# A routing table made in smaller pieces beside four expert tiles instead of three

## The chip, the cores and the metric

The kernel runs on one core of one Trainium2 chip. The metric is device microseconds from launch to end. The engines are called PE (TensorE, the matrix engine), DVE (VectorE), ACT (ScalarE), POOL (GpSimd) and SP (SyncE, which here only issues DMAs). Each takes its own instructions in order.

## The reference

A spectral layer on 8 sequences of 2496 x 256, then a mixture of 8 experts, one expert per token, 19968 tokens in all:

```
X  = rfft(x, axis=1)
Yr = Xr @ w_r - Xi @ w_i + b_r ;  Yi = Xr @ w_i + Xi @ w_r + b_i
Y  = soft-shrink of both by 0.01 ;  y = irfft(Y)           # 8 x 2496 x 256
logits = y @ w_gate ;  expert = argmax(logits) ;  g = softmax(logits)[expert]
out[token] = g * (relu(y @ w1[expert]) @ w2[expert])       # w1 256x1024, w2 1024x256
```

## The kernel before, in words

**Spectral part** (`spectral`, 80 iterations, ten for each of 8 batches). An iteration multiplies, shrinks and transforms one slice of frequencies of its batch (`fwd_b`, `halves`, `mix`, `shrink`, `inv_b`; one copy `k`, L349, in each), and in four of the ten also runs three steps of the last transform of the batch before (`inv_a`, matmuls `pz` and `py`). In the last batch there is no next batch to begin. `finish_last` then runs `inv_a` for the last batch alone.

**Routing** (`route`). For each half of a batch some 25 small DVE operations and a few others find every token's expert and its row in `xs_dram`, a list sorted by expert; eleven scatters by POOL (L637) then write the tokens there. This is a Python generator: the code between two `yield`s is a piece. The generators wait in `self.jobs`, one behind the other, and `tick(n)` runs the next n pieces of the first one at the place where it is called. `send(n)` does the same with the scatters, each behind a one-element copy by POOL (`pace`, L568).

**Tables** (`table`). An expert tile is 256 rows of `xs_dram` of one expert. `table(0)` chooses, from the counts without the last two batches, five early tiles (`EARLY`); it is queued after the second iteration of the last batch. `table(1)` lists the remaining tiles when all tokens are routed. Each is a chain of some 36 DVE operations on 128 x 8 values, two small groups of matmuls (`pn`, `pq`; `pl` for the second) and a cast into `tabs`, from which SP reads a tile's row, expert and whether the expert changed (`word`, L748).

**Expert tiles** (`step(t)` = `up(t)`, then `down(t)`). `up` multiplies the tile's tokens by `w1` into four groups `ph`; ACT makes `hh` of each (L863) and DVE `hl` (L864), the two halves of an exact split. After each group one piece of `upright(t + 1)` is run, which turns the next tile's tokens: for early tiles by PE (`px`, L828), for the others by a DVE transpose (L832) of `xq`, then a cast `xh` by ACT and a subtraction `xl` by DVE. `down` multiplies by `w2` into `po`, half by half, and DVE writes `o` (L904), which POOL scatters to `out`. In its first half `down(t)` splits the `w2` of tile t + 1 (`split2`, L813 on ACT and L814 on DVE) and then asks for that of tile t + 2; in its second half the same with `w1` (`split1`, L798, L799). `load(t)` asks for a tile's rows: four DMAs `xq` and one `xr` on SP. A weight DMA is skipped by a condition where the expert did not change; at the first tile of a table it is always made.

Before the change steps 0 to 2 run in `finish_last`, and `up` and `down` call `tick(3)` after each group of `ph` and each half while `t < 3`: 18 pieces for each tile. Then `experts_rest` asks for the rows of tiles 5 and 6, and in the loop from tile 3 on for those of tile t + 4 ahead of step t. The order of the code is the order on all four engines PE, ACT, DVE and SP (`manual_schedule`).

Of the kernel before, what the change touches and what calls it, by code (L numbers as in the profile page):

```python
# [98 lines left out]
class Kernel:  # L99
# [443 lines left out]
    def finish_last(self, late):  # L543
        for i in range(GH + 1):
            self.inv_a(self.nb - 1, i)
            if self.early and i >= 2:
                next(self.fill, None)
            if self.early and i == GH - 1:
                for _ in self.upright(0):
                    pass  # L550
            self.tick(4)
            if i > GH // 2 + 1:
                self.pace(self.yb[0:1, 0, 8:9])
                self.send(1)
        self.jobs.append(self.table(1))
        if not self.early:
            self.tick(100)
            return
        for _ in self.fill:
            pass  # L560
        for t in range(3):
            self.step(t)
        self.tick(100)
        self.send(100)
# [86 lines left out]
    def table(self, last):  # L651
        nc, rt = self.nc, self.rt
        tcol, base = self.tcol, self.base

        def small(nm):
            return rt.tile([128, E], F32, tag=nm, name=nm)

        def prefix(src):
            a, b = small("pfa"), small("pfb")
            nc.vector.tensor_copy(a, src)  # L660
            for d in (1, 2, 4):
                nc.vector.tensor_copy(b[:, :d], a[:, :d])
                nc.vector.tensor_add(b[:, d:], a[:, d:], a[:, :E - d])
                a, b = b, a
            return a

        p = self.psi.tile([128, 512], F32, tag="yo", name="pn")
        nc.tensor.matmul(p[:, :E], self.ones_b, self.carry_b, start=True, stop=True)
        n8 = small("n8")
        nc.vector.tensor_copy(n8, p[:, :E])  # L670
        cnt = small("cnt")
        half = (TT - 1) / 2
        nc.vector.tensor_scalar(out=cnt, in0=n8, scalar1=half if last else -half, scalar2=1.0 / TT,
                                op0=ALU.add, op1=ALU.mult)
        nc.vector.tensor_scalar_add(cnt, cnt, ROUND)
        nc.vector.tensor_scalar_add(cnt, cnt, -ROUND)
        yield
        te, ge, st0, ind = small("te"), small("ge"), small("st0"), small("ind")
        if last:
            nc.vector.tensor_sub(cnt, cnt, self.used)  # L680
        end = prefix(cnt)
        yield
        nc.vector.tensor_sub(st0, end, cnt)
        fin = rt.tile([128, 5], F32, tag="fin", name="fin")
        for j in range(2):
            nc.vector.tensor_tensor(out=te, in0=tcol[:, j:j + 1].broadcast_to((128, E)), in1=end, op=ALU.is_ge)
            if j == 0:
                nc.vector.tensor_copy(ge, te)
            nc.vector.tensor_reduce(out=fin[:, j:j + 1], in_=te, axis=AX.X, op=ALU.add)
        yield  # L690
        nc.vector.tensor_scalar_min(fin[:, 0:2], fin[:, 0:2], float(E - 1))
        nc.vector.tensor_tensor(out=fin[:, 2:3], in0=fin[:, 0:1], in1=fin[:, 1:2], op=ALU.is_gt)
        nc.vector.tensor_max(fin[:, 1:2], fin[:, 2:3], tcol[:, 2:3])
        nc.vector.tensor_scalar(out=te, in0=st0, scalar1=tcol[:, 0:1], scalar2=-1.0, op0=ALU.subtract, op1=ALU.mult)
        nc.vector.scalar_tensor_tensor(out=ind, in0=te, scalar=0.0, in1=ge, op0=ALU.is_ge, op1=ALU.subtract)
        yield
        nc.vector.tensor_add(te, te, self.used)
        nc.vector.tensor_copy(fin[:, 4:5], end[:, E - 1:E])
        if not last:
            nc.vector.tensor_scalar(out=st0, in0=st0, scalar1=-1.0, scalar2=float(self.early),  # L700
                                    op0=ALU.mult, op1=ALU.add)
            nc.vector.tensor_scalar_max(st0, st0, 0.0)
            nc.vector.tensor_tensor(out=self.used, in0=st0, in1=cnt, op=ALU.min)
        nc.vector.tensor_scalar_add(n8, n8, -float(TT))
        nc.vector.tensor_scalar_mul(te, te, float(TT))
        nc.vector.tensor_tensor(out=st0, in0=te, in1=n8, op=ALU.min)
        nc.vector.tensor_sub(te, te, st0)
        yield
        nc.vector.tensor_mul(te, te, ind)
        nc.vector.tensor_reduce(out=fin[:, 3:4], in_=te, axis=AX.X, op=ALU.add)  # L710
        nc.vector.tensor_add(st0, st0, base)
        nc.vector.tensor_mul(st0, st0, ind)  # L712
        nc.vector.tensor_reduce(out=fin[:, 2:3], in_=st0, axis=AX.X, op=ALU.add)
        for _ in range(6):
            yield
        yield "pe"
        p = self.psi.tile([128, 512], F32, tag="yo", name="pq")
        for i, j in enumerate((0, 1, 2, 4)):
            nc.tensor.matmul(p[0:1, i * 128:(i + 1) * 128], fin[:, j:j + 1], self.ident, start=True, stop=True)
        yield  # L720
        nc.vector.tensor_copy(self.tabs[last], p[0:1, :].rearrange("p (a b) -> p a b", a=4))
        if last:
            lap = rt.tile([128, 128], F32, name="lap")
            nc.vector.tensor_copy(lap, fin[:, 3:4].broadcast_to((128, 128)))
            for _ in range(4):
                yield
            p = self.psi.tile([128, 512], F32, tag="yo", name="pl")
            nc.tensor.matmul(p[:, 0:128], lap, self.ident, start=True, stop=True)
            for h in range(2):
                nc.vector.tensor_scalar(out=self.drop[:, :, h], in0=p[:, 0:128], scalar1=tcol[:, 3 + h:4 + h],  # L730
                                        scalar2=float(OOB), op0=ALU.is_gt, op1=ALU.mult)
# [112 lines left out]
    def up(self, t, work=()):  # L844
        work = iter(work)
        nc = self.nc
        xh, xl = self.xts.pop(t)
        h1, l1 = self.ws.pop((t, 1))
        hh = self.w2p.tile([128, 8, TT], F32R, tag="hh", name="hh")
        hl = self.w2p.tile([128, 8, TT], F32R, tag="hl", name="hl")  # L850
        for f2 in range(4):
            p = (self.psb if self.psb and f2 % 2 else self.psa).tile([128, 2, TT], F32, tag="h", name="ph")
            for i in range(2):
                f = f2 * 2 + i
                m = 0
                for c in range(2):
                    for a, v in ((h1, xh), (l1, xh), (h1, xl)):
                        nc.tensor.matmul(p[:, i, :], a[:, c, f * 128:(f + 1) * 128], v[:, c, :],  # L858
                                         start=m == 0, stop=m == 5)
                        m += 1  # L860
            s = slice(f2 * 2, f2 * 2 + 2)
            with self.tc.high_priority():
                nc.scalar.activation(hh[:, s, :], p, AF.Relu)  # L863
                nc.vector.scalar_tensor_tensor(out=hl[:, s, :], in0=p, scalar=0.0, in1=hh[:, s, :],  # L864
                                               op0=ALU.max, op1=ALU.subtract)
            next(work, None)
            if t < 3:
                self.tick(3)
                self.pace(hh.bitcast(F32)[0:1, f2 * 2, 0:1])
                self.send(1)  # L870
        self.hs[t] = (hh, hl)

    def down(self, t):
# [13 lines left out]
        for h in range(2):  # L887
# [8 lines left out]
                nc.tensor.matmul(p, hh[:, f, hs], w2[:, f].rearrange("p a d -> p (a d)"), start=f == 0, stop=f == 7)  # L896
            for _ in work[h]:
                pass
            if t < 3:
                self.tick(3)  # L900
                self.send(2)
            part = self.w2p.tile([128, D], F32, tag="part", name="part", bufs=2)
# [30 lines left out]

    def experts_rest(self, late):
        late.enter_context(self.tc.manual_schedule(engines={mybir.EngineType.Activation, mybir.EngineType.DVE}))
        t0 = 3 if self.early else 0
        if not t0:
            for _ in self.fill:
                pass
# [43 lines left out]
```

## Time and profile before

| what | value |
|---|---|
| timed runs, median of 3 | 1584.38 us (1581.14 to 1585.53) |
| profiled execution, its own time | 1573.86 us |
| its span, first to last instruction | 1572.1 us |
| busy share PE / DVE / ACT / POOL | 97 / 79 / 69 / 35% |
| mean granted clock of the PE | 0.988 |
| spectral part, last batch, `finish_last` | to about 588, to about 617 us |
| expert tiles | from about 617 us on, 82 of them |

The profiled execution was 10.5 us faster than the median of the timed ones, so a prediction is made as a difference. The page gives busy time by engine and in 40 slices; the granted clock is a share of 2.4 GHz. In the profile's groups a line can stand for many instructions. A wait is put down to what was released last.

### The profile page before, as it was taken

The numbers are of one execution on the slowest core, as the hardware profiler recorded it, in microseconds if no ns is written. First come the engines' busy times: TensorE is split into PE (matmuls) and PEld (weight loads), VectorE is DVE, ScalarE is ACT, GpSimd is POOL, SyncE is SP. The second block draws the span as 40 slices with busy tenths as digits, with TensorE's granted clock in tenths as the row PEclk, the third lists the DMA queues.
The fourth block names the chain that finished last, engine by engine and source line by source line (L and its number), as shares of the span: only waits on it lengthen the run. The fifth ranks groups of instructions, "written<-read, shape, count | busy, mean of one in ns | idle before, by whom it ended". The sixth has DMA issues, their size and how long they took to land. (4 is left out here: it accounts for less than half of the span.)

```text
span 1572.1 us, 36022 instructions
## 1 busy us (share of the span) xinstructions
PE 1523.4 (97%) x10954; PEld 1405.3 (89%) x10954; DVE 1242.6 (79%) x2680; ACT 1078.8 (69%) x2257; POOL 542.4 (35%) x532
## 2 busy tenths in 40 slices
PE   6999999999999898999999999999999999999996
PEld 3899999999999788889999999999999999999996
DVE  3678777777878777788888888888888888888886
ACT  2667677767777566566767677676767676777765
POOL 1002433525253353623343333333333333333333
PEclk8999999999999999999999999999999999999998
DMA  8764545646453113243214123214123123223110
GB/s 245 227 191 125 159 142 146 178 116 186 122 166 109 59 55 124 79 103 101 48 46 102 45 52 93 55 42 103 44 50 96 48 48 96 52 73 71 42 49 20
DMA packets 182964, 153.56 MB, mean 98 GB/s; under 512 B 120474, under 2 KB 154176, under 8 KB 182509
## 3 DMA queue, kind: packets, MB, share of 16 engines
q1 hardware_dynamic: 162829, 107.17, 26.7%
q0 software_dynamic: 19936, 44.04, 8.6%
q8 instruction: 89, 1.46, 0.4%
q14 instruction: 110, 0.90, 0.2%
HBM read 243.07 MB, written 66.37 MB: 197 GB/s over the span
## 5 line engine op out<-in xcount | busy, mean ns | idle before, releaser
L906 POOL DMA_INDIRECT out<-o,row x154 | 302.5, 1965 | 572.3 <-DVE o L904 531.8
L896 PE MATMUL po<-h,hh 128*128 128x512 f32 x1312 | 462.4, 396 | 0.0
L858 PE MATMUL ph<-xh,h 128*128 128x256 f32 x1312 | 371.5, 283 | 0.9 <-ACT h L798 0.7
L858 PE MATMUL ph<-xh,l 128*128 128x256 f32 x1312 | 371.0, 283 | 0.7 <-DVE l L799 0.7
L858 PE MATMUL ph<-xl,h 128*128 128x256 f32 x1312 | 370.6, 282 | 0.0
L863 ACT ACTIVATE hh<-ph 128x512 fp32r<-128x512 f32 x328 | 196.0, 598 | 239.7 <-PE ph L858 222.3
L864 DVE SCALAR_TENSOR_TENSOR hl<-ph,hh 128x512 fp32r<-128x512 f32 x328 | 226.8, 691 | 138.5 <-ACT hh L863 127.7
L893 PE MATMUL po<-h,hl 128*128 128x256 f32 x1148 | 322.2, 281 | 2.5 <-DVE st L712 1.3
L896 PEld LDWEIGHTS po<-h,hh 128*128 128x128 f32 x1312 | 241.6, 188 | 44.7 <-issue 0.6
L858 PEld LDWEIGHTS ph<-xh,l 128*128 128x128 f32 x1312 | 250.8, 191 | 4.8 <-DVE l L799 1.1
L858 PEld LDWEIGHTS ph<-xh,h 128*128 128x128 f32 x1312 | 250.6, 191 | 2.1 <-ACT h L798 1.3
L858 PEld LDWEIGHTS ph<-xl,h 128*128 128x128 f32 x1312 | 250.8, 191 | 0.0
L893 PEld LDWEIGHTS po<-h,hl 128*128 128x128 f32 x1148 | 217.1, 189 | 7.0 <-DVE st L712 1.6
L799 DVE TENSOR_TENSOR l<-r,h 128x512 fp32r<-128x512 f32 x332 | 206.9, 684 | 3.2 <-ACT h L798 2.5
L814 DVE TENSOR_TENSOR h<-r,h 128x512 fp32r<-128x512 f32 x332 | 207.1, 685 | 2.4 <-ACT h L813 2.4
L637 POOL DMA_INDIRECT xs_dram<-yb,pos x176 | 178.2, 1013 | 73.9 <-issue 49.9
L813 ACT CAST h<-r 128x512 fp32r<-128x512 f32 x332 | 180.4, 618 | 1.8 <-DMA r<-moe_w 1.8
L798 ACT CAST h<-r 128x512 fp32r<-128x512 f32 x332 | 180.7, 618 | 1.4 <-DMA r<-moe_w 1.4
L370 DVE SCALAR_TENSOR_TENSOR y<-v,r 64x256 f32<-64x256 f32 x320 | 134.2, 419 | 6.9 <-ACT r L364 1.6
L326 DVE TENSOR_TENSOR su<-re,pb 128x256 f32<-128x256 f32 x80 | 33.7, 421 | 86.9 <-ACT sh L325 42.7
L394 PE MATMUL pz<-iw,z 128*120 128x136 f32 x704 | 97.4, 282 | 0.8 <-ACT z L386 0.7
L903 ACT ACTIVATE part<-po,xr 128x256 f32<-128x256 f32 x154 | 73.1, 475 | 36.1 <-PE po L896 35.9
(183 smaller groups left out, 2813.2 us busy)
## 6 DMA issues: line engine op xcount, KB each, us to landing
r<-moe_w SPq DMA_DIRECT2D x178, 512.0 KB
r<-moe_w SPq DMA_DIRECT2D x632, 128.0 KB
spec_dram<-ae SPq DMA_DIRECT2D x88, 240.0 KB
t<-spec_dram SPq DMA_DIRECT2D x160, 128.0 KB
xq<-xs_dram SPq DMA_DIRECT2D x312, 64.0 KB
x<-x SPq DMA_DIRECT2D x40, 384.0 KB
x<-x SPq DMA_DIRECT2D x40, 84.0 KB
xs_dram<-yb,pos POOLq DMA_INDIRECT x176
```

The source lines that it names most:

```text
L370: nc.vector.scalar_tensor_tensor(out=y[q * 64:q * 64 + 64, kp, :], in0=u[h, q, :], scalar=LAM, in1=r[h, q, :], op0=ALU.add, op1=ALU.min)
L637: i = nc.gpsimd.indirect_dma_start(out=self.xs[:, :], out_offset=bass.IndirectOffsetOnAxis(ap=pos[:n, g:g + 1], axis=0), in_=y[:n, g, 0:XW ...
L798: nc.scalar.copy(hi[:, c, s], v)
L799: nc.vector.tensor_sub(lo[:, c, s], v, hi[:, c, s])
L813: nc.scalar.copy(hi[:, s, :], v)
L814: nc.vector.tensor_sub(lo[:, s, :], v, hi[:, s, :])
L858: nc.tensor.matmul(p[:, i, :], a[:, c, f * 128:(f + 1) * 128], v[:, c, :], start=m == 0, stop=m == 5)
L863: nc.scalar.activation(hh[:, s, :], p, AF.Relu)
L864: nc.vector.scalar_tensor_tensor(out=hl[:, s, :], in0=p, scalar=0.0, in1=hh[:, s, :], op0=ALU.max, op1=ALU.subtract)
L893: nc.tensor.matmul(p[:, :D], hl[:, f - 1, hs], w2[:, f - 1, 0, :], start=False, stop=False)
L896: nc.tensor.matmul(p, hh[:, f, hs], w2[:, f].rearrange("p a d -> p (a d)"), start=f == 0, stop=f == 7)
L906: i = nc.gpsimd.indirect_dma_start(out=self.out[:, :], out_offset=bass.IndirectOffsetOnAxis(ap=at[h], axis=0), in_=o[:, h, :], in_offset=N ...
```

## The change

`table` gets more `yield`s: six ahead of its first operation, one between every one to three operations of the chain, and one in each step of the prefix sum, which becomes a generator itself. Nothing of what is computed changes. So that the table still ends in time, a fourth step is run in `finish_last`, `up` and `down` call `tick` while `t < 4`, and `experts_rest` starts at tile 4.

```diff
@@ finish_last
-        for t in range(3):
+        for t in range(4):
             self.step(t)
@@ table
             for d in (1, 2, 4):
+                yield
                 nc.vector.tensor_copy(b[:, :d], a[:, :d])
...
+        for _ in range(6):
+            yield
         p = self.psi.tile([128, 512], F32, tag="yo", name="pn")
...
                                 op0=ALU.add, op1=ALU.mult)
+        yield
         nc.vector.tensor_scalar_add(cnt, cnt, ROUND)
...
-        end = prefix(cnt)
+        end = yield from prefix(cnt)
...
             nc.vector.tensor_reduce(out=fin[:, j:j + 1], in_=te, axis=AX.X, op=ALU.add)
-        yield
+            yield
         nc.vector.tensor_scalar_min(fin[:, 0:2], fin[:, 0:2], float(E - 1))
         nc.vector.tensor_tensor(out=fin[:, 2:3], in0=fin[:, 0:1], in1=fin[:, 1:2], op=ALU.is_gt)
+        yield
         nc.vector.tensor_max(fin[:, 1:2], fin[:, 2:3], tcol[:, 2:3])
...
@@ up, down
-            if t < 3:
+            if t < 4:
                 self.tick(3)
@@ experts_rest
-        t0 = 3 if self.early else 0
+        t0 = 4 if self.early else 0
```

(The further `yield`s in `table` are of the same kind. Lines of the changed kernel from the table on are 1 to 12 higher.)

What stands where, first on DVE in the last batch of the spectral part, at the start of `table(0)` (L670 to L689 are the table, the others the spectral work of that iteration: `zl` of the transform, `sl` and `y` of the slice). Before:

```order
L330 TENSOR_TENSOR sl_7518<-su_7520,sh_7517 128x2x128
L670 COPY n8_7545<-pn_7543 128x8
L673 TENSOR_SCALAR cnt_7547<-n8_7545 128x8
L675 TENSOR_SCALAR cnt_7547<-cnt_7547 128x8
L676 TENSOR_SCALAR cnt_7547<-cnt_7547 128x8
L660 COPY pfa_7555<-cnt_7547 128x8
...
L686 TENSOR_TENSOR te_7551<-tcol_79,pfb_7556 128x8
L689 TENSOR_REDUCE fin_7565<-te_7551 128x1
L370 SCALAR_TENSOR_TENSOR y_7584<-v_7500,r_7539 64x256 x2
```

Now:

```order
L370 SCALAR_TENSOR_TENSOR y_7556<-v_7500,r_7539 64x256 x2
L673 COPY n8_7592<-pn_7590 128x8
L676 TENSOR_SCALAR cnt_7594<-n8_7592 128x8
L679 TENSOR_SCALAR cnt_7594<-cnt_7594 128x8
L680 TENSOR_SCALAR cnt_7594<-cnt_7594 128x8
L357 TENSOR_TENSOR v_7613<-pm_7598,k_7550 128x512
L400 TENSOR_TENSOR zl_7619<-pz_7615,zh_7618 120x272
L400 TENSOR_TENSOR zl_7626<-pz_7622,zh_7625 120x272
L660 COPY pfa_7643<-cnt_7594 128x8
L663 COPY pfb_7644<-pfa_7643 128x1
L664 TENSOR_TENSOR pfb_7644<-pfa_7643 128x7
L326 TENSOR_TENSOR su_7663<-re_7662,pb_7655 128x256
```

The seventeen rows that stood ahead of `y` are now behind it, in groups with the iterations' own work between them.

On DVE in tile 1, at the start of `table(1)` (`hl` is the tile's own work, L680 to L713 the table's). Before:

```order
L864 SCALAR_TENSOR_TENSOR hl_9178<-ph_9219,hh_9177 128x512
L841 TENSOR_TENSOR xl2_9200<-px_9194,xh2_9199 128x512
L680 TENSOR_TENSOR cnt_9211<-cnt_9211,used_74 128x8
...
L695 SCALAR_TENSOR_TENSOR ind_9238<-te_9235,ge_9236 128x8
L864 SCALAR_TENSOR_TENSOR hl_9178<-ph_9265,hh_9177 128x512
L697 TENSOR_TENSOR te_9235<-te_9235,used_74 128x8
...
L713 TENSOR_REDUCE fin_9250<-st0_9237 128x1
L864 SCALAR_TENSOR_TENSOR hl_9178<-ph_9295,hh_9177 128x512
```

Now:

```order
L876 SCALAR_TENSOR_TENSOR hl_9174<-ph_9227,hh_9173 128x512
L673 COPY n8_9244<-pn_9242 128x8
L676 TENSOR_SCALAR cnt_9246<-n8_9244 128x8
L876 SCALAR_TENSOR_TENSOR hl_9174<-ph_9252,hh_9173 128x512
L679 TENSOR_SCALAR cnt_9246<-cnt_9246 128x8
...
L664 TENSOR_TENSOR pfb_9275<-pfa_9274 128x7
L826 TENSOR_TENSOR h2_9301<-r20_8470,h2_9301 128x2x256
```

Two of the table's rows stand between the tile's pieces of `hl`, the others in groups of three to eight among the splits of the weights; the last twelve come in tile 2, and the cast into `tabs` (`tab1`) at the end of tile 2 instead of tile 1.

On SP after the last weights of the early tiles (`r10`, `r11` are `w1`, `r20`, `r21` are `w2`, `xq` a tile's rows; `xq_9658` and `xq_9837` are those of tile 5). Before:

```order
L786 DMA r11_8473<-moe_w1 128x1024
L763 DMA xq_9658<-xs_dram 32x8x64
...
L763 DMA xq_9674<-xs_dram 32x8x64
...
L763 DMA xq_9690<-xs_dram 32x8x64
...
L786 DMA r20_8474<-moe_w2 128x4x256
L786 DMA r21_8475<-moe_w2 128x4x256
L786 DMA r10_8472<-moe_w1 32x1024
```

Now:

```order
L798 DMA r11_8469<-moe_w1 128x1024
L798 DMA r20_8470<-moe_w2 128x4x256
L798 DMA r21_8471<-moe_w2 128x4x256
L798 DMA r10_8468<-moe_w1 32x1024
...
L798 DMA r11_8469<-moe_w1 32x1024
...
L775 DMA xq_9837<-xs_dram 32x8x64
...
L775 DMA xq_9885<-xs_dram 32x8x64
```

The ten weight DMAs of tile 5, which stood behind the rows of tiles 5 to 7, now stand ahead of the rows of tiles 5 to 8.

## Rows read from the trace of the kernel before

**Rows 1.** The page: busy time by engine, share of the span, instructions.

```profile
PE 1523.4 (97%) x10954; PEld 1405.3 (89%) x10954; DVE 1242.6 (79%) x2680; ACT 1078.8 (69%) x2257; POOL 542.4 (35%) x532
```

**Rows 2.** Busy time by stretch: from:to in us, its length, busy us of each engine (instructions), granted clock of the PE, DMA share, GB/s. The first is an iteration of the batch before the last, the next three of the last batch (from one copy `k` to the next); then tiles 1, 2, 3 and 4, each from one second `o` to the next.

```profile
472.54:481.69 9.15, 9.15 (x74) 8.66 (x73) 7.43 (x25) 6.62 (x20) 0.00 (x0) 1.00 0.21 58
516.10:525.19 9.09, 4.13 (x36) 3.90 (x34) 5.15 (x16) 2.90 (x8) 6.56 (x9) 0.95 0.46 139
525.19:537.19 12.00, 11.44 (x73) 10.83 (x74) 9.85 (x44) 6.27 (x17) 3.61 (x6) 0.75 0.08 26
537.19:547.91 10.72, 10.05 (x81) 9.36 (x79) 7.35 (x20) 6.53 (x19) 0.00 (x0) 1.00 0.00 0
...
630.14:648.97 18.83, 15.83 (x95) 12.46 (x93) 15.65 (x57) 7.80 (x16) 13.91 (x17) 0.91 0.28 87
648.97:660.49 11.52, 11.51 (x79) 10.61 (x80) 9.48 (x17) 7.81 (x15) 8.91 (x11) 1.00 0.20 60
660.49:672.29 11.80, 11.80 (x86) 11.09 (x85) 8.97 (x17) 7.95 (x15) 3.13 (x3) 1.00 0.48 101
672.29:686.54 14.25, 12.83 (x86) 11.23 (x85) 9.85 (x17) 8.14 (x15) 1.96 (x2) 1.00 0.70 186
```

**Rows 3.** The timeline: start, duration, engine, line, operation, in brackets the idle time of the engine just before it and what ended it. Around `table(0)`; last, a stretch as in rows 2.

```profile
519.97 0.37 ACT L324 COPY re<-pb 128x256 f32<-128x256 f32 x1 [3.41 <-PE pz L394]
523.91 0.16 DVE L670 COPY n<-pn 128x8 f32<-128x8 f32 x1
525.62 0.57 PE L408 MATMUL py<-zh,gh 120*117 120x272 f32 x1 [5.39 <-ACT k L349]
529.95 0.16 DVE L711 TENSOR_TENSOR st<-st,base 128x8 f32<-128x8 f32 x1
...
526.00:528.00 2.00, 2.00 (x11) 2.00 (x11) 1.80 (x10) 0.91 (x3) 0.99 (x1) 0.50 0.00 0
```

**Rows 4.** The timeline of tile 1 around `table(1)`; last, two stretches.

```profile
638.15 0.39 PE L893 MATMUL po<-h,hl 128*128 128x256 f32 x1 [1.25 <-DVE hl L864]
639.08 0.17 DVE L709 TENSOR_TENSOR te<-te,ind 128x8 f32<-128x8 f32 x1
640.56 0.58 PE L893 MATMUL po<-h,hl 128*128 128x256 f32 x1 [1.29 <-DVE st L712]
648.12 0.67 DVE L721 CAST tab<-pq 1x512 int32<-1x512 f32 x1
648.72 0.20 DVE L724 COPY lap<-fin 128x128 f32<-128x128 f32 x1
...
640.00:642.00 2.00, 1.44 (x5) 0.92 (x6) 2.00 (x4) 0.77 (x2) 1.66 (x2) 0.59 0.19 61
642.00:644.00 2.00, 2.00 (x10) 1.09 (x9) 0.91 (x2) 0.00 (x0) 1.50 (x1) 0.55 0.21 66
```

**Rows 5.** The timeline of a steady tile, from its start at the second `o` of the tile before to its own.

```profile
731.65 0.48 DVE L904 SCALAR_TENSOR_TENSOR o<-po,xr,part 128x256 f32<-128x256 f32 x1
733.41 0.70 DVE L832 STREAM_TRANSPOSE xf<-xq 128x512 f32<-128x512 f32 x1
734.15 0.62 ACT L838 CAST xh<-xf 128x512 fp32r<-128x512 f32 x1
735.05 0.60 ACT L863 ACTIVATE hh<-ph 128x512 fp32r<-128x512 f32 x1 [0.28 <-PE ph L858]
736.29 0.68 DVE L841 TENSOR_TENSOR xl<-xf,xh 128x512 fp32r<-128x512 f32 x1
737.12 0.69 DVE L864 SCALAR_TENSOR_TENSOR hl<-ph,hh 128x512 fp32r<-128x512 f32 x1 [0.15 <-ACT hh L863]
737.24 0.28 PE L893 MATMUL po<-h,hl 128*128 128x256 f32 x1
738.65 0.28 PE L893 MATMUL po<-h,hl 128*128 128x256 f32 x1
743.01 0.48 DVE L904 SCALAR_TENSOR_TENSOR o<-po,xr,part 128x256 f32<-128x256 f32 x1
```

**Rows 6.** The timeline of SP's queue (start, time until the last of the group was issued) and of ACT's waits for the weights of tile 5; the last two rows are SP's in a steady tile.

```profile
672.59 8.57 SPq L786 DMA_DIRECT2D r<-moe_w  x10
677.72 3.44 SPq L786 DMA_DIRECT2D r<-moe_w  x6
680.59 1.14 ACT L813 CAST h<-r 128x512 fp32r<-128x512 f32 x2 [1.76 <-DMA r<-moe_w]
681.97 1.87 SPq L763 DMA_DIRECT2D xq<-xs_dram  x4
684.08 1.66 ACT L798 CAST h<-r 128x512 fp32r<-128x512 f32 x3 [0.78 <-DMA r<-moe_w]
...
739.31 6.13 SPq L786 DMA_DIRECT2D r<-moe_w  x10
746.06 1.86 SPq L763 DMA_DIRECT2D xq<-xs_dram  x4
```

**Rows 7.** The timeline: POOL's last scatter of the spectral part, SP's loads of the early tiles' rows, and the PE's first use of them.

```profile
593.91 0.90 POOL L637 DMA_INDIRECT xs_dram<-yb,pos  x1 [0.30 <-issue]
599.07 5.42 SPq L758 DMA_DIRECT2D xw<-xs_dram  x5
613.86 0.60 PE L828 MATMUL px<-ident,xw 128*128 128x128 f32 x4
```

More of the change, by code (lines that the diff above doesn't have):

```diff
@@ L689, in table @@
             nc.vector.tensor_reduce(out=fin[:, j:j + 1], in_=te, axis=AX.X, op=ALU.add)
-        yield
+            yield
         nc.vector.tensor_scalar_min(fin[:, 0:2], fin[:, 0:2], float(E - 1))
         nc.vector.tensor_tensor(out=fin[:, 2:3], in0=fin[:, 0:1], in1=fin[:, 1:2], op=ALU.is_gt)
+        yield
         nc.vector.tensor_max(fin[:, 1:2], fin[:, 2:3], tcol[:, 2:3])
         nc.vector.tensor_scalar(out=te, in0=st0, scalar1=tcol[:, 0:1], scalar2=-1.0, op0=ALU.subtract, op1=ALU.mult)
+        yield
         nc.vector.scalar_tensor_tensor(out=ind, in0=te, scalar=0.0, in1=ge, op0=ALU.is_ge, op1=ALU.subtract)
@@ L698, in table @@
         nc.vector.tensor_copy(fin[:, 4:5], end[:, E - 1:E])
+        yield
         if not last:
@@ L702, in table @@
             nc.vector.tensor_scalar_max(st0, st0, 0.0)
+            yield
             nc.vector.tensor_tensor(out=self.used, in0=st0, in1=cnt, op=ALU.min)
         nc.vector.tensor_scalar_add(n8, n8, -float(TT))
+        yield
         nc.vector.tensor_scalar_mul(te, te, float(TT))
         nc.vector.tensor_tensor(out=st0, in0=te, in1=n8, op=ALU.min)
+        yield
         nc.vector.tensor_sub(te, te, st0)
@@ L710, in table @@
         nc.vector.tensor_reduce(out=fin[:, 3:4], in_=te, axis=AX.X, op=ALU.add)
+        yield
         nc.vector.tensor_add(st0, st0, base)
         nc.vector.tensor_mul(st0, st0, ind)
+        yield
         nc.vector.tensor_reduce(out=fin[:, 2:3], in_=st0, axis=AX.X, op=ALU.add)
@@ L898, in down @@
                 pass
-            if t < 3:
+            if t < 4:
                 self.tick(3)
```

## The prediction

> **What bounds the kernel now.** I read the page first. TensorE (PE) is busy for 97% of the span, so an edit counts only where it opens or closes a gap on PE [rows 1]. Then the busy time by stretch. The steady expert tiles show the floor: from one last write of `o` (L904) to the next, 731.65 to 743.01, 11.36 us pass [rows 5]. Below I call the moment at which tile t's last `o` starts T(t). Against this floor three places stand out, and the change touches all of them.
>
> The first is the last batch of the spectral part, where table(0) is made. An iteration, counted from one copy of `k` (L349) to the next, takes 9.15 us with the PE busy for all of it in the batch before, and 12.00 and 10.72 us in the last batch [rows 2]. VectorE (DVE) works off the table there, from the copy `n` at 523.91 us to the operation at 529.95 and a little beyond. The PE has a gap of 5.39 us up to 525.62 and then is granted 0.50 of its clock, the level of 1.2 GHz [rows 3]. But look at the order of events: the PE's last matmul before the gap starts by 520, and ScalarE (ACT) is already late at 519.97, four microseconds before the table's first DVE row. So this gap did not start with the table, and I count it apart.
>
> The second is tile 1, with table(1): 18.83 us, DVE busy for 15.65 of them [rows 2]. Here the cause is plain. Two pieces of `hl` (L864) stand behind runs of table rows, and the PE waits 1.25 us for the one, 1.29 us under the name of a table row for the other, and then is granted 0.59 and 0.55 of its clock on the mean of two stretches [rows 4]. The third is tile 4, 14.25 us: ScalarE waits for the weights of tile 5, which SP began to issue at 672.59 us only, after T(3), since the rows of tiles 5 to 7 stand ahead of them in its queue [rows 2, 6].
>
> **The change part by part.**
>
> *Table(0) in pieces.* The same 36 DVE rows are issued, each some 0.17 us, 0.2 us from one to the next where each needs the one before [rows 3, 4]. They now stand between the pieces of four iterations, in groups of two to eight rows. What they add, 7 us over four iterations of about 9, fits: DVE is busy for 7.43 us of such an iteration [rows 2]. The gain at the two iterations is (12.00 - 9.15) + (10.72 - 9.15) = 4.4 us. In the iteration before them the PE stands idle for 9.09 - 4.13 = 4.96 us [rows 2]. These began before the table and I do not count them; with them the gain would be 9.4 us, the upper end. The lower end is nothing: DVE does the same work, and the routing behind it is pushed into later, shorter iterations.
>
> *The scatters behind it.* The routing of batch 6 now comes later by the table's added turns, so that ten of its scatters stand in one burst at the end of the spectral part instead of five. The burst is hidden: the early tiles' rows were loaded at 599.07 us, after the last scatter (593.91 us), and the PE first used them at 613.86 us. That is 14.8 us of cover, against 5.42 us for issuing the five loads [rows 7]. If the spectral part ends 9 us earlier and the burst does not, the cover is still 5.8 us. Cost 0.
>
> *Table(1) in pieces.* In tile 1 the PE is idle for 18.83 - 15.83 = 3.0 us [rows 2]. The half clock behind its two waits cost, at 0.59 and 0.55 of the clock over 2 us each, another 2 x 0.41 + 2 x 0.45 = 1.7 us [rows 4]. So at most 4.7 us can come back. Is there room for it on DVE? Twelve of the table's rows move to tile 2 (12 x 0.17 = 2.0 us), and the cast of the table and the copy `lap` (0.67 + 0.20 us) with them, 2.9 us [rows 4]. That leaves tile 1 with 15.65 - 2.9 = 12.75 us of DVE work against 15.83 - 1.7 = 14.1 us of PE work, and tile 2 with 9.48 + 2.9 = 12.4 us against the PE's 11.51 and the table's last matmuls, which come along [rows 2]. DVE is thus close to the bound in tile 2, and I leave about 1 us lost in small waits there: 3.7 us gained. The lower end is 1.25 us, one of the two waits; a loss would need table rows in longer runs than before, and the runs get shorter.
>
> *The fourth tile called early.* Step 3 itself costs the same: it has two score buffers for `ph` in place of four, and tile 2, which had two, took 11.52 us against 11.80 us of tile 3, which had four [rows 2]. What moves is its queue work. In its second half it asks for the weights of tile 5, ten DMAs on SP, and the rows of tiles 5 to 8 come behind them. Two things follow. The stall of tile 4, 14.25 - 11.36 = 2.9 us, goes, since the weights are asked for on time. But the rows of tile 5 are now issued after T(3), and DVE's transpose of them (L832) stands in its queue right behind the first `hl` of tile 4, with three more pieces of `hl` behind it. In the steady state this transpose starts at T + 1.76 us (733.41), and the PE uses the second `hl` at T + 5.59 (737.24) and the last one at T + 7.00 (738.65) [rows 5]. From a late transpose at T + X the chain to the last `hl` is 0.70 + 0.62 + 0.60 + 0.69 + 0.68 + 0.69 = 3.98 us (transpose, ACT's cast and `hh`, `hl`, `xl`, `hl`), so the PE is late by X - 3.0 us.
>
> X is in no row. In the steady state the ten weight DMAs are through SP at T + 2.43 (739.31 + 6.13) and the four loads of rows at T + 3.05 to 4.91 [rows 6]; but there the weights are skipped. Where they really were fetched, six issues took 3.44 us and the rows came 0.81 us later; by these, eight from T - 0.5 end at T + 4.1 and the rows are issued by T + 6.8. The nearest row for landing is the last part of `w1`: issued by 681.16, its consumer released at 684.08, 2.9 us [rows 6]. So X lies between 7.8 and 9.7 and I take 8.7: late by 5.7 us. A gap of that size brings the half clock, as the 5.39 us gap did [rows 3]; I take the 1.7 us that it cost in tile 1. Tile 4 thus changes by 5.7 + 1.7 - 2.9 = 4.5 us for the worse. Lower end: rows there the moment they are issued, X = 4.9 and no drop of the clock, a gain of 1.0 us. Upper end 11.6 us (below).
>
> By the Trainium skill (*DMA: Bandwidth & Descriptors*, Anatomy of one DMA) a DMA costs about 2.0 us and its bytes at 436 GB/s; for 64 KB this is an estimate of 2.2 us, the lateness would be 0.7 us less and the time 1580.1. No row here shows a lone load of this size.
>
> Sum: 4.4 + 3.7 - 4.5 = 3.6 us less. The profiled execution took 1573.86 us (span 1572.1), 10.5 us under the median of the timed runs, 1584.38; taken off that median, **1580.8 us**. This kernel's runs differ by some 0.3% (1581.14 to 1585.53), which is 4.8 us, so I forecast no change that can be told for sure.
>
> **The rivals.**
>
> *Faster: the gap at 520 us is the table's as well.* For it: it is seen only in this iteration, the one with the table's matmul `pn` in the PE's queue, whose buffer is freed by the table's first DVE row at 523.91. Against it: ACT was late before. Then the gain is 9.4 + 3.7 - 4.5 = 8.6 us: 1575.8 us.
>
> *Slower: tile 5's rows come only when the weights have landed.* The place is the transpose in tile 4, the price one microsecond for each that X grows, and it decides from X = 12.3 on, where 4.4 + 3.7 is used up. For it: the fetch of both weights took from 672.59 to 684.08, 11.5 us [rows 6]; counted from an issue at T - 3.7, as in the steady tile (739.31 against 743.01), they are there at T + 7.8. If the rows then take as long as the second half of `w2` did, 8.0 us (680.59), X is 15.8, tile 4 loses 11.6 us and the kernel 3.5 us: 1587.9 us. Against it: those 8 us were for 1 MB with other loads beside it, not for 64 KB.
>
> A rule speaks for this rival: by the Trainium skill (*DMA: Bandwidth & Descriptors*, Queues, rings and completion order) each DMA engine takes the descriptors of one queue in ring order, and SP has one queue; the 2 MB of weights would be ahead of the rows. The late landing of `w2` in this trace fits that but does not prove it.
>
> *The change does not do what it says.* In the new order up to eight table rows still stand together, and the routing follows in shorter iterations, where DVE is nearer to its limit. Then the first gain is nothing, the second 1.25 us, tile 4 costs its 4.5 us: 3.25 us lost, 1587.6 us.
>
> **How the numbers follow.** Chances: forecast 0.45, its own range 1577 to 1585; faster rival 0.26; late rows 0.17; no gain from the pieces 0.12. Faster by over 0.3% means under 1579.6: nearly all of the first rival and 0.13 of the forecast, 0.36. Slower by over 0.3% means over 1589.1: half of the third case, some of the last, and a little of the forecast, 0.18. The rest is 0.46. The range reaches from halfway between the first rival and the same with the rows of tile 5 early (9.4 + 3.7 + 1.0 = 14.1 us less, 1570.3), 1573, to a little past the two cases above 1587, 1589.5.
>
> **What would show it.** The stretches: the two iterations with table(0) near 9.2 us, tiles 1 and 2 together near 18.83 + 11.52 - 3.7 = 26.7, tile 4 near 14.25 + 4.5 = 18.8 us with DVE idle before the transpose and a drop of the granted clock. Right but mis-sized is tile 4 at 13 or 26. Wrong is the forecast if tile 4 shows no wait for the rows, if the iterations of the last batch stay at 11 to 12 us, or if the gap of 5 us before them is gone too.

## The result, and the profile after

The changed kernel took 1593.93 us (median of 6 runs, 1589.92 to 1598.27); the kernel before took 1581.81 us beside it. The ratio is 1.0075 (95% interval 1.006 to 1.009): 12 us slower, where 3.6 us less were forecast. The profiled execution took 1598.27 us, the longest of the six; its span is 1596.4 us.

First the page's line of busy times, which answers to [rows 1]: the PE is now busy for 96% of a longer span, and DVE did no more work than before.

```profile
PE 1532.7 (96%) x10953; PEld 1412.5 (88%) x10954; DVE 1241.2 (78%) x2680; ACT 1078.3 (68%) x2257; POOL 539.6 (34%) x528
```

The busy time by stretch, as in [rows 2]: three iterations of the last batch, then from its last copy `k` to T(0), then tiles 1 to 4.

```profile
518.71:529.42 10.71, 5.05 (x38) 4.54 (x36) 3.73 (x8) 2.78 (x8) 6.56 (x9) 0.78 0.39 119
529.42:540.10 10.68, 10.11 (x64) 9.74 (x64) 7.08 (x21) 6.03 (x18) 3.86 (x6) 0.74 0.09 28
540.10:548.82 8.72, 8.58 (x73) 8.35 (x72) 8.12 (x35) 6.25 (x19) 0.00 (x0) 1.00 0.01 2
587.40:643.97 56.57, 44.58 (x301) 40.24 (x301) 33.76 (x95) 32.45 (x80) 23.98 (x30) 0.88 0.36 107
643.97:662.99 19.02, 15.35 (x99) 13.99 (x97) 12.83 (x43) 7.79 (x16) 14.56 (x17) 0.91 0.27 86
662.99:676.54 13.55, 12.29 (x82) 10.26 (x80) 11.29 (x29) 8.10 (x17) 8.49 (x11) 1.00 0.20 61
676.54:688.20 11.66, 11.53 (x79) 10.63 (x80) 9.38 (x18) 7.45 (x15) 2.17 (x2) 1.00 0.22 75
688.20:706.84 18.64, 13.38 (x85) 12.15 (x84) 9.47 (x17) 7.87 (x15) 3.02 (x2) 0.91 0.61 143
```

Tile 4 is as forecast (18.64 us; 18.8 forecast). The fourth row is not. In the kernel before, this stretch of `finish_last` and tile 0 was:

```profile
582.38:630.14 47.76, 41.65 (x290) 37.08 (x289) 33.55 (x96) 32.02 (x80) 20.16 (x27) 0.96 0.38 116
```

It is now 8.8 us longer, and the forecast had its only change, the later scatters, at a cost of nothing. Of the 8.8 us, 5.9 are idle time of the PE (11.99 against 6.11 us) and 2.9 are longer busy time, with a granted clock of 0.88 instead of 0.96. What happens there, in the timeline of the changed kernel:

```profile
594.09 2.38 PE L394 MATMUL pz<-iw,z 128*120 128x136 f32 x16 [0.79 <-ACT z L386]
595.12 0.39 ACT L399 CAST zh<-pz 120x272 fp32r<-120x272 f32 x1 [0.58 <-PE pz L394]
598.42 0.39 ACT L399 CAST zh<-pz 120x272 fp32r<-120x272 f32 x1 [2.92 <-remote]
601.27 0.39 ACT L399 CAST zh<-pz 120x272 fp32r<-120x272 f32 x1 [2.46 <-PE pz L394]
602.80 0.99 POOL L637 DMA_INDIRECT xs_dram<-yb,pos  x1 [0.30 <-issue]
604.10 0.90 POOL L637 DMA_INDIRECT xs_dram<-yb,pos  x1 [0.30 <-issue]
604.12 0.39 ACT L399 CAST zh<-pz 120x272 fp32r<-120x272 f32 x1 [2.46 <-remote]
607.01 0.67 ACT L409 COPY yb<-py 117x272 f32<-117x272 f32 x2 [2.50 <-remote]
607.45 0.57 PE L408 MATMUL py<-zh,gh 120*117 120x272 f32 x1 [6.17 <-ACT yb L409]
```

The first four `pz` are through the PE by 596.5. ACT needs each of them for one copy `zh` and should take them one after the other, but gets the second at 598.42 and the next two at steps of 2.85 us, while POOL issues scatters 1.3 us apart. I call this late signals: the matmul is done in the trace, and the engine that waits for it learns of it microseconds later. (The profile models where a matmul ends. But the PE has gone on to its next matmuls, `py`, by 596.56, and the trace has the semaphore that ACT waits for raised at 598.40, 601.25 and 604.10 us: the signal is late, and not ACT.) The last scatter is issued at 604.10, and the PE goes on at 607.45. "Remote" means that the profile does not tell what ended the wait.

The same pattern stands in tile 1: the last matmul of the first half `po` is through by 651.8, ACT waits for it from then on and is let go at 656.58, and by then the PE and DVE stand still too. The scatters around it start 1.3 to 2.0 us apart.

```profile
651.11 0.64 PE L908 MATMUL po<-h,hh 128*128 128x512 f32 x2
...
653.91 0.40 PE L908 MATMUL po<-h,hh 128*128 128x512 f32 x1
655.00 0.99 POOL L637 DMA_INDIRECT xs_dram<-yb,pos  x1 [0.30 <-issue]
656.58 0.47 ACT L915 ACTIVATE part<-po,xw 128x256 f32<-128x256 f32 x1 [4.77 <-remote]
657.61 0.39 PE L870 MATMUL ph<-xh,h 128*128 128x256 f32 x1 [3.31 <-ACT part L915]
```

And tile 4, in SP's queue, on DVE and on the PE:

```profile
694.33 1.89 SPq L775 DMA_DIRECT2D xq<-xs_dram  x4
697.94 0.71 DVE L844 STREAM_TRANSPOSE xf<-xq 128x512 f32<-128x512 f32 x1 [7.82 <-DMA xq<-xs_dram]
699.28 0.58 PE L905 MATMUL po<-h,hl 128*128 128x256 f32 x1 [5.26 <-DVE hl L876]
```

X is 697.94 - 688.20 = 9.7 us (8.7 taken).

### The profile page after: what moved, and what is told of

It reads as the page before. It is cut to its first block, busy times and chain, and to the rows that moved or that the text cites. A ratio compares the mean times of both kernels' runs of the same rounds, so it can differ in the third digit from the quotient of the medians.

```text
span 1596.4 us, 36011 instructions
## 1 busy us (share of the span) xinstructions
PE 1532.7 (96%) x10953; PEld 1412.5 (88%) x10954; DVE 1241.2 (78%) x2680; ACT 1078.3 (68%) x2257; POOL 539.6 (34%) x528
```

## The experiments

All 18 runs in one table. "Against before" is the difference of medians within a set of runs that shared a chip, and behind it the ratio on record with its 95% interval; the two are not worked out alike and differ by up to 2 us. The stretches, in us, are from each kernel's own profile: eight iterations of the last batch, last `k` to T(0), tiles 1 and 2, tile 4. Kernels of different sets ran on different chips, which matters below. In `after_again` the batch is counted from a `k` that was itself over 3 us late (524.68 us), so its 63.67 is too short to compare.

| kernel | before in its set | against before (ratio, interval) | batch | k to T(0) | 1+2 | 4 |
|---|---|---|---|---|---|---|
| before | | | 66.28 | 47.76 | 30.36 | 14.26 |
| changed | 1581.8 | +12.1 (1.0075, 1.006-1.009) | 68.69 | 56.57 | 32.57 | 18.64 |
| t0_block | 1578.4 | +5.1 (1.0032, 1.0017-1.0047) | 65.54 | 50.35 | 32.29 | 19.55 |
| delay | 1578.4 | +10.3 (1.0078, 1.006-1.0095) | 69.62 | 54.88 | 32.46 | 13.81 |
| spaced | 1578.4 | +2.3 (1.002, 1.0008-1.0033) | 60.50 | 51.98 | 25.73 | 19.10 |
| rows5 | 1578.4 | +6.0 (1.004, 1.0027-1.0053) | 67.95 | 53.29 | 30.28 | 11.36 |
| t0_early | 1563.7 | -0.7 (0.9999, 0.9985-1.0012) | 59.93 | 44.10 | 25.77 | 18.67 |
| before_spaced | 1563.7 | +7.8 (1.0044, 1.0029-1.006) | 64.46 | 46.60 | 28.26 | 14.20 |
| best2 | 1563.7 | +8.9 (1.0049, 1.0032-1.0066) | 60.61 | 53.08 | 26.42 | 12.20 |
| best3 | 1563.7 | +5.7 (1.0029, 1.0018-1.004) | 61.55 | 46.49 | 26.43 | 12.51 |
| before_again | 1584.1 | (1578.6, one run) | 65.00 | 50.08 | 33.54 | 14.19 |
| after_again | 1584.1 | +9.1 (1.007, 1.0047-1.0093) | 63.67 | 53.62 | 32.35 | 19.51 |
| t0_early_rows5 | 1584.1 | -1.7 (0.9997, 0.9981-1.0014) | 63.32 | 50.58 | 32.32 | 11.36 |
| delay_again | 1584.1 | +6.4 (1.0043, 1.0028-1.0059) | 69.86 | 56.90 | 33.46 | 14.60 |
| lean | 1581.8 | +10.2 (1.0057, 1.0035-1.0079) | 74.33 | 45.23 | 32.32 | 18.63 |
| best4_dense | 1581.8 | +5.6 (1.0024, 1.0009-1.0039) | 75.89 | 46.87 | 32.35 | 11.36 |
| best4 | 1581.8 | -9.4 (0.9933, 0.9916-0.9951) | 68.83 | 44.71 | 26.41 | 12.63 |
| best3_again | 1564.3 | +4.2 (1.0024, 1.0011-1.0038) | 61.42 | 46.50 | 26.42 | 12.02 |
| best4_again | 1564.3 | +9.7 (1.0065, 1.0043-1.0086) | 68.72 | 44.77 | 26.44 | 11.57 |
| before_third | 1564.3 | (1567.8, one run) | 64.67 | 44.12 | 29.75 | 14.02 |

**Is it the late scatters or the pieces?** `delay` issues nothing new; it only puts the routing of batch 6 later:

```diff
 # kernel before, table
+        for _ in range(0 if last else 19):
+            yield
         p = self.psi.tile([128, 512], F32, tag="yo", name="pn")
```

> The kernel before, with 19 empty pieces ahead of table(0): the table stays in one block, but the routing of batch 6 and its scatters come as late as in the changed kernel. Scatters, and buffer yb: 8 to 11 us lost from the last batch to the end of tile 0, time 1590 to 1593 against 1582 before. DVE: nothing is lost, since no operation is added or split, 1582.

> The kernel before with 19 empty pieces ahead of table(0), once more. If the wait for the buffer yb alone carries the cost of late scatters: +5 to +9 us on any chip. If the PE's late signals carry it: +12 us where the gap at 520 us is seen, and under 4 us where it is not.

Busy time by stretch of `delay`, last `k` to T(0):

```profile
585.90:640.78 54.88, 44.90 (x300) 40.49 (x299) 33.86 (x95) 32.68 (x80) 24.18 (x30) 0.91 0.36 110
```

The order alone costs 7 us here and 3 us in the batch, with the table in one block. Without a choice of stretches it is plainer still: T(0) is at 630.14 and 632.03 us in the two profiles `before` and `before_again`, at 643.97 and 641.97 in the changed kernel's two, and at 640.78 and 643.75 in those of `delay` and `delay_again`. So most of the changed kernel's loss comes without its change, and the pieces on DVE fall as the main cause. In time the first run met its expectation (+10.3), but the second, at +6.4, lies where the buffer alone was to put it, though its timeline has the late signals (ACT waits 3.2, 3.2 and 3.9 us for `zh` after the last iteration). The times of `delay` do not tell the two ways apart. The converse is `t0_block` (table(0) as before, the rest as changed):

```diff
-                self.jobs.append(self.table(0))
+                self.jobs.append(self.table_block(0))   # the generator of the kernel before
```

> The changed kernel, with table(0) as it was before (in few pieces); table(1) in pieces and the fourth early step stay. Three theories of the lost time between the last batch and the end of tile 0 (11 us in the two profiles). Scatters: the scatters of batch 6 come later behind a table of 19 more pieces, POOL then issues some ten of them with nothing between, and meanwhile the PE's end-of-matmul signals reach ACT late; then this kernel is back at the shorter run of scatters: from the last copy k to the end of tile 0 48 us instead of 56.6, time 1583 to 1586. Buffer yb: ACT may not overwrite yb before the late scatters have read it; the same times. DVE: the pieces themselves crowd the short iterations; then at most the 2.4 us of the last batch come back, 1591.

50.35 us, T(0) at 633.13, and 5 us over before, about what tile 4 loses (19.55 against 14.26 us). `t0_early` keeps the pieces and brings the scatters back in time:

```diff
-            if late and self.early and s == 1:
+            if self.early and it == n - 11:
                 self.jobs.append(self.table(0))
```

> The changed kernel, with table(0) queued two iterations earlier (after the last but one batch, ahead of the routing of batch 6 by more pieces than were added), so that the scatters of batch 6 come as in the kernel before: runs of five at the end, not ten. If the late scatters cost the time, by whichever way: from the last copy k to T(0) 48 to 50.5 us instead of 56.6, time 6 to 10 us under the changed kernel, +2 to +6 against before. If the pieces on DVE cost it: within 2 us of the changed kernel, +10 to +12 against before.

44.10 us and no difference to before. This set ran on another chip, on which before itself took 1564 us, so 44.10 is to be held against `before_third` (44.12, below), not against 56.57; and since neither the changed kernel nor `delay` ran on such a chip, what the late scatters cost there is not known. The test on a chip of the first kind is `t0_early_rows5` (below): there T(0) is at 632.39 us, where `before_again` on the same chip has 632.03 and the changed kernel, `after_again`, 641.97.

**What do the scatters do?** `spaced` puts a fill on POOL behind each scatter:

```diff
                     ... reason="a few rows per slot")
+                self.paced = nc.gpsimd.memset(self.spacer, 0.0)   # 128 x 528
+                tc.add_manual_dep(self.paced.ins, i.ins.name, ...)
                 yield
```

> The changed kernel, with a fill of 128 x 528 words on POOL (about 0.53 us) behind every scatter of the routing, so that no two follow each other at 1.3 us. Scatters: the PE's signals come on time; the gap of 5.7 us in the iteration at 519 to 528 us, the gaps of 2.0 and 6.2 us after the last iteration and that of 3.3 us in tile 1 shrink by more than half, 1579 to 1586. Buffer yb: the scatters end later by 10 times 0.6 us and the gaps after the last iteration grow, 1597 to 1601. DVE: no change, 1594.

Its timeline after the last iteration, then three iterations with table(0) by stretch:

```profile
584.08 1.78 ACT L400 CAST zh<-pz 120x272 fp32r<-120x272 f32 x4 [0.58 <-PE pz L395]
599.84 0.90 POOL L638 DMA_INDIRECT xs_dram<-yb,pos  x1 [0.18 <-issue]
602.25 0.39 ACT L410 COPY yb<-py 117x272 f32<-117x272 f32 x1 [7.56 <-DMA xs_dram<-yb,pos]
602.69 0.58 PE L409 MATMUL py<-zh,gh 120*117 120x272 f32 x1 [6.82 <-ACT yb L410]
```

```profile
515.92:519.68 3.76, 3.76 (x35) 3.76 (x34) 3.24 (x8) 2.66 (x8) 3.40 (x6) 1.00 0.44 138
519.68:528.42 8.74, 8.37 (x69) 7.95 (x68) 7.11 (x23) 5.96 (x19) 8.00 (x14) 1.00 0.25 78
528.42:537.58 9.16, 8.93 (x72) 8.42 (x72) 8.56 (x34) 6.33 (x19) 5.36 (x9) 1.00 0.15 45
```

The time, 1580.7 us, is what the theory of the scatters had. With some 1.75 us from one scatter to the next the late signals are gone: four copies `zh` in 1.78 us where they were spread over 9 us, tile 1 at 14.15 us, and no gap at 520. But both theories were half right: with the signals on time the PE runs on and then meets the other wait, ACT's for the buffer `yb`, which the last scatter still reads. Either way the PE goes on some 3 us after that scatter (607.45 - 604.10; 602.69 - 599.84). The wait for `yb` by itself shows in `best2` and `best3`, which share a chip and the fills and differ only in when table(0) is queued: ACT waits 9.2 us for a scatter in the one and 2.4 in the other, the stretch falls from 53.08 to 46.49 us as expected, the time by 3.2 us (4 to 7 expected). In tile 3 (18.13 us) the fills made POOL late, and ACT waited 5.8 us for POOL to read `hh`. A third buffer `yb`, which would take that wait alone away, wasn't tried.

`before_spaced` spaces the scatters of batches 0 to 6 in the kernel before (the same edit, under `if b < self.nb - 1`):

> The kernel before, with the POOL fill behind every scatter of batches 0 to 6 (the last batch's are left as they were). If scatters that follow each other at 1.3 us hold back the PE's signals, the gap of 5.4 us at 520 us is theirs and not the table's: the three iterations with table(0) (9.09, 12.0 and 10.7 us) lose 5 to 8 us in sum, while the scatters end later, so that the wait for the buffer yb after the last iteration grows by 3 to 6 us; in all 0 to 5 us faster than before. If the gap were the table's: it stays at 4 us or more, and the time is 3 to 6 us over before.

There is no gap in the iteration at 520 (it takes 3.77 us). But this set, too, had before at 1564 us, and `before_third` (below) has none there either without any fill, so this run does not show that spacing removes it; `spaced` does, on a chip where `delay` and `t0_block` have it. The next iteration takes 17.15 us: the PE waits 5.4 us for DVE, which has the table in one block. The three iterations together lose 0.4 us instead of 5 to 8, and the time is 7.8 us over before: not as expected.

**Do the late signals differ from chip to chip?** Two profiles of the kernel before answer that.

> The kernel before once more, for a profile beside those of this set (its time on the last chip was 1564 us, 15 to 18 us less than on the two before). If the PE's late signals behind dense scatters differ from chip to chip: where the time is near 1564 us the gap of 5.4 us at 520 us and those of 1.4 and 0.9 us at 593 us are gone or below 2 us, and the stretch from the last k to T(0) takes 44 to 45 us instead of 47.8; where the time is near 1580 us they are there.

> The kernel before, for one more profile on the chip of this set. Where its time is about 1580 us: gaps of 3.5 us or more on the PE at 520 to 530 and at 593 to 600 us. Where it is about 1564 us: none over 2 us at either place, if the late signals are what sets the two kinds of chip apart.

> The changed kernel once more. If the late PE signals carry most of its loss and this chip shows them: +11 to +13 us against before, as at first. If this chip does not show them: only tile 4 (+4.4 us) and the wait for the buffer yb remain, +5 to +10 us.

The changed kernel took 9.1 us more than before here, less than the 11 to 13 expected. The timeline after the last iteration of `before_again` (before at 1584 us in its set):

```profile
587.76 2.38 PE L394 MATMUL pz<-iw,z 128*120 128x136 f32 x16 [0.83 <-ACT z L386]
590.91 0.99 POOL L637 DMA_INDIRECT xs_dram<-yb,pos  x1 [0.30 <-issue]
592.21 1.00 POOL L637 DMA_INDIRECT xs_dram<-yb,pos  x1 [0.31 <-issue]
592.96 0.39 ACT L399 CAST zh<-pz 120x272 fp32r<-120x272 f32 x1 [2.47 <-issue]
593.51 0.90 POOL L637 DMA_INDIRECT xs_dram<-yb,pos  x1 [0.30 <-issue]
596.24 0.58 PE L408 MATMUL py<-zh,gh 120*117 120x272 f32 x1 [4.43 <-ACT yb L409]
```

and of `before_third` (before at 1564 us), the same program, with one of its iterations by stretch:

```profile
586.01 2.38 PE L394 MATMUL pz<-iw,z 128*120 128x136 f32 x16 [0.75 <-ACT z L386]
587.04 1.78 ACT L399 CAST zh<-pz 120x272 fp32r<-120x272 f32 x4 [0.58 <-PE pz L394]
587.88 0.99 POOL L637 DMA_INDIRECT xs_dram<-yb,pos  x1 [0.30 <-issue]
589.18 0.99 POOL L637 DMA_INDIRECT xs_dram<-yb,pos  x1 [0.30 <-issue]
590.48 0.90 POOL L637 DMA_INDIRECT xs_dram<-yb,pos  x1 [0.30 <-issue]
```

```profile
518.46:534.24 15.78, 12.21 (x77) 11.22 (x76) 11.89 (x54) 6.61 (x18) 7.17 (x12) 0.78 0.20 61
```

The same scatters at the same 1.3 us, and on this chip the signals come on time (k to T(0) 44.12 against 50.08 us). Only here does one see what the table in one block costs: an iteration of 15.78 us. The gap there is 3.48 us, more than the 2 us expected, but it is ended by DVE's `zl` and not by a late signal. Each of these sets ran on a chip of its own, so whether it is the chip that differs, or something else of the set, is not shown.

**Tile 4.** `rows5` asks for the rows of tile 5 ahead of step 3:

```diff
         for t in range(4):
+            if t == 3:
+                self.tick(100)
+                self.send(100)
+                self.load(self.early)
             self.step(t)
```

(The loop behind it then begins with the rows of tile 6.)

> The changed kernel, with the rows of tile 5 asked for on SP at the start of step 3, ahead of the weights of tile 5. If the late rows make tile 4 long, as predicted: the transpose starts within 3 us of T(3), tile 4 takes 11.4 to 12 us instead of 18.6, time 1587. If the weights of tile 5 were its bound as well: tile 4 stays at 14 us or more, 1590.

SP's queue and DVE's transpose in `rows5`:

```profile
671.62 2.05 SPq L779 DMA_DIRECT2D xq<-xs_dram  x4
685.85 0.70 DVE L848 STREAM_TRANSPOSE xf<-xq 128x512 f32<-128x512 f32 x1
```

Tile 4 is at 11.36 us, the floor: the late rows were its only limit, as predicted. The time is 1584.4 us, 6 over before. Some of it comes back elsewhere: tile 3 takes 13.72 us (11.66 in the changed kernel), tiles 5 and 8 take 12.73 and 12.62 us.

**A version that beats both?** `t0_early_rows5` has both edits. `lean` has these two:

```diff
-        for _ in range(6):                       # both places in table
+        for _ in range(6 if last else 0):
             yield
-            spare = 1 if late else 0
+            spare = 2 if late else 0
```

`best4_dense` is `lean` with the rows early. `best4` also has the fills, and in `up`:

```diff
-                self.pace(hh.bitcast(F32)[0:1, f2 * 2, 0:1])
```

`best2` is `spaced` with the rows early and this line out, `best3` the same with the early table.

> The changed kernel with table(0) queued two iterations earlier and the rows of tile 5 asked for ahead of its weights. The two losses found are independent: the scatters come as in the kernel before, and tile 4 falls from 18.7 to about 11.5 us, so 5 to 8 us under before. If the loss only moves (weights late for tiles 5 and 6 behind the rows): tiles 5 to 8 together 3 us over four times 11.36, and 2 to 4 us under before.

> The changed kernel, in which table(0) has no empty pieces and each place in the last batch runs one piece more, so that the scatters of batch 6 come in time (runs of four at the end, not ten) while the table stays in pieces. If late scatters cost the time: from the last k to T(0) 47 to 51 us, 5 to 9 us under the changed kernel, +2 to +6 against before (tile 4 stays long). If crowding on DVE costs it: the same as the changed kernel or worse, since more pieces stand in each iteration, +11 to +15.

> The last kernel with the rows of tile 5 ahead of its weights. Tile 4 falls from 18.6 to 11.4 us and about 3 us of that come back in tiles 5 to 8: -3 to +2 against before.

> The last kernel with the POOL fill behind every scatter and without the copies of hh on POOL. If scatters at 1.3 us hold back the PE's signals: the iterations with table(0) take 3.8, 8.7 and 9.2 us instead of 9 to 12, no gap over 1.5 us in the tiles, 6 to 14 us under the last kernel and 5 to 12 us under before. If spacing only moves the wait to the buffer yb: within 3 us of the last kernel.

> The changed kernel with three edits: the POOL fill behind every scatter, the rows of tile 5 ahead of its weights, and no one-element copies of hh on POOL in the expert tiles (ACT waited 5.8 us for such a copy behind POOL's queue in tile 3 of the run with the fill). Theory of the scatters: tile 1 near 14, tile 3 near 12, tile 4 near 11.5 us; 8 to 14 us under before. If the fills make POOL late for the rows of tile 5 (its loads wait for the last scatter): tile 4 at 14 to 18 us and 2 to 6 us under before.

> The last kernel with table(0) also queued two iterations earlier. The last scatter of batch 6 comes some 8 us earlier, and with it the wait of ACT for the buffer yb, 7.6 us in the run with the fill: from the last copy k to T(0) 45 to 48 us, and 4 to 7 us less than the kernel without this edit. If that wait is not set by the last scatter: no difference.

> The changed kernel with the POOL fill, table(0) queued two iterations earlier, the rows of tile 5 ahead of its weights and no copies of hh on POOL, once more; it took +4.6 us against a before of 1564 us on the one chip of that time. Its stretches from the first of the iterations with table(0) to T(8) summed to some 5 us less than those of the kernel with one piece more at each place. If the late PE signals differ from chip to chip: where before takes about 1580 us, 10 to 18 us under before; where it takes about 1564 us, again +3 to +7.

> The kernel with the fill and one piece more at each place of the last batch, once more (-9.4 us against a before of 1582 us). Where before takes about 1580 us: -7 to -12; where it takes about 1564 us: +3 to +9, as the other kernels with the fill.

Most of these expectations were missed. `t0_early_rows5` is no faster than before: T(0) and tile 4 are as expected, but tiles 1 and 2 keep their late signals (32.32 us) and tiles 5 to 8 take 47.98 us, 2.5 over four times the floor. `best4_dense` is 5.6 us over before and `best2` 8.9 over. `best3_again`, at +4.2, is as expected where before takes 1564 us, and `best4_again`, at +9.7, a little over.

On one chip, `best4` is 15 us under `best4_dense`, from which it differs by the spacing and the copies, whose shares were not told apart: tiles 1 and 2 fall from 32.35 to 26.41 us and the batch by 7, though two of the three iterations stay long (3.76, 11.29 and 16.13 us; 3.8, 8.7 and 9.2 expected). It is 9.4 us faster than before. `lean` shows that scatters in time shorten the end (45.23 us) but that a piece more at each place lengthens the batch (74.33): the miss of its expectation (10.2 us over before, where +2 to +6 were forecast from the scatters). Where before took 1564 us, all kernels with fills were slower than it, by 4 to 10 us. `best4` was the only one run on both kinds: 1572 and 1574 us, against a before of 1582 and 1564. So no version was shown to beat before on both; `best4` did on the one chip with late signals on which it ran.

## Why the prediction was wrong

**The scatters behind table(0), "cost 0": the step that failed.** I followed them to the loads of the early tiles' rows [rows 7], found 14.8 us of cover, and stopped. They have two other followers: the buffer `yb` that they read and the transform of the last batch writes, and whoever waits for the PE while they are issued. The order alone cost 6 to 10 us in time (`delay`, twice), against a forecast of 0. How much of that is the buffer and how much the late signals stays open. The signs that I had named for being wrong did not come: tile 4 waits for its rows, the two iterations take 10.68 and 8.72 us, and the gap before them is still there. I had named none for the stretch where the cost fell. A wait of ACT for a scatter stood in the timeline of the kernel before, and I had not followed it:

```profile
593.15 0.39 ACT L409 COPY yb<-py 117x272 f32<-117x272 f32 x1 [1.03 <-DMA xs_dram<-yb,pos]
```


**Table(0) in pieces, 4.4 us: not gained.** The two iterations that I counted gained 3.3 us (19.40 instead of 22.72), but the one ahead of them lost 1.6, and the five behind them take 38.58 us instead of 34.47, since the routing now falls there: the PE waits for DVE's `sb` twice, in the changed kernel's timeline (before only once, 2.15 us at 568.93):

```profile
567.15 0.22 PE L617 MATMUL pr<-sb,ltri 117*117 117x8 bf16 x1 [2.17 <-DVE sb L613]
578.93 0.17 PE L617 MATMUL pr<-sb,ltri 117*117 117x8 bf16 x1 [2.89 <-DVE sb L613]
```

That was the lower end of the forecast, for the reason given there. The check that the rows fit was none: 7.43 us of DVE and a fourth of 7 make 9.2 in an iteration of 9.15. To count the 5 us at 520 apart was right: they are late signals, and go with the spacing, not with the table. But little of them could have been gained: without them, in `before_third`, the block makes the iteration behind longer, and the two take 19.54 us together instead of 21.09. With the signals on time the pieces do what they are for (8.74 and 9.16 us in `spaced`; 17.15 with the block in `before_spaced`), and the batch takes 60.61 us in `best2` against 64.46 in `before_spaced`, on one chip with the same fills: 3.9 us for the 4.4 forecast.

**Table(1), 3.7 us: not gained here.** Tiles 1 and 2 took 32.57 us (26.7 forecast, 30.35 before). The two waits of [rows 4] were the table's, as I had read them: `before_third`, with the signals on time, has them as well.

```profile
631.51 0.39 PE L893 MATMUL po<-h,hl 128*128 128x256 f32 x1 [1.25 <-DVE hl L864]
633.92 0.38 PE L893 MATMUL po<-h,hl 128*128 128x256 f32 x1 [1.44 <-DVE hl L864]
```

The changed kernel has neither, but a new wait of 3.31 us in tile 1, for a late signal behind the last batch's scatters (657.61, above). In `spaced`, `t0_early` and `best4`, where the signals are on time, the two tiles take 25.7 to 26.4 us, 4.0 less in `t0_early` (25.77) than in `before_third` (29.75). So this term was right where the signals come on time, and what I had left out of it is the scatters again.

**The fourth step: right.** Tile 4 took 18.64 us (18.8 forecast), X 9.7 (8.7). The PE is idle for 5.3 us of it (5.7 taken) and busy 2.0 us longer than the floor, at a granted clock of 0.91 (1.7 taken). The parts of X were off both ways: the rows were issued by T(3) + 8.0 us (4.9 to 6.8 taken), and from the last issue of `xq` (694.33 + 1.89) to the transpose there are 1.7 us (2.9 taken). The estimate from the Trainium skill (*DMA: Bandwidth & Descriptors*, Anatomy of one DMA), whose fit is for DMAs that POOL issues, was 2.2, so the trace is a little under it. The rival of rows that wait for the whole weights, X = 15.8, fell.

**The rivals.** The time lay above all of them. The rows behind the weights came nearest as a number (1587.9) and fell in tile 4; "the change does not do what it says" (1587.6) had the first gain right, that of nothing, but not the cost of the scatters.

**The sum.** The stretches of the two profiles (batch, last `k` to T(0), tiles 1 and 2, tile 3, tile 4) differ by +2.4, +8.8, +2.2, -0.1 and +4.4 = 17.7 us, where the forecast had -4.4, 0, -3.7, 0 and +4.5. The medians differ by 12.1 only: the profiled execution of the changed kernel was the longest of its six, with a steady tile of 11.41 us instead of 11.36, and that of the kernel before 8 us under its median.

## What to carry to other kernels

When a step is moved, list every reader of what it reads and writes, the buffers that it frees among them, not only the transfer that it feeds. A wait whose releaser the profile does not name is a question to settle before its time is given to the neighbour; see whether it goes with another queue's activity. Where DMAs are issued close together on POOL, try to spread them, and compare on more than one chip: here it gained where the signals came late, and all kernels with fills lost where they did not.

## What the runs showed of the hardware

Behind scatters 1.3 to 2.0 us apart the PE's end signals reached ACT up to 5 us late (651.8 to 656.58 in tile 1), after the last iteration, with scatters 1.3 us apart, at steps of 2.85 us. With a fill of POOL behind each scatter, some 1.75 us apart after the last iteration, they were on time (`spaced`, `best4`). Sets on different chips differ in it: the same program takes 1578 to 1584 us where it is seen and 1564 us where it is not. What holds the signals back stays open, and whether the fill or the spacing takes them away; the runs show only what goes with it.
